# First-stage products issued in pairs on borrowed PSUM banks, and the middle column of x taken once a batch

## The chip, the cores and the metric

The kernel runs on one core of one Trainium2 chip. The metric is the device time of one execution in microseconds (us). The kernel before has a median of 1967.06 us over three runs (1964.94 to 1967.59). One more execution was recorded by the hardware profiler, and all times below that carry a position ("at 344.28") are microseconds from the start of that recorded span.

## The reference

```python
def _attn_ref(x):                 # x: 8 batches x 3008 rows x 256 columns, float32
    X = np.fft.fft(x, axis=1)
    X = np.fft.fft(X, axis=2)
    return X.real.astype(np.float32)

def _moe_ref(x, w_in, w_out):     # the 24064 rows of the result, w_in 256x2048, w_out 2048x256
    h = x @ w_in
    g = h * np.cos(h)
    return (g @ w_out).astype(np.float32)
```

The real part of a two-dimensional Fourier transform of each batch is followed by a two-layer network whose activation is h times cos(h). Everything is float32.

## The kernel before

The transform over the 3008 rows is split as 47 x 64. For each batch there is a **first stage**: the input is loaded in four parts of eight values of the row index modulo 64 (`load_x`, L140, four to six DMAs each on SyncE's queue), GpSimd folds columns d and 256-d into sums and differences (`fold`, L211; on VectorE for batch 0, ScalarE copies column 0 and the middle column 128), and `first_half` (L232) multiplies one chunk of four index values by the DFT matrix `L`. One chunk gives a PSUM tile `pz` of 128 x 512: its lower 64 partitions come from the sums ("even"), its upper 64 from the differences ("odd"). Since the weights have only 64 columns, the even and the odd products use different column halves of the array. A third, tiny product puts the middle column of x, which belongs to the even part, into the four odd columns that would be zero; it goes first. Chunk 0 has a column with weights of its own and needs six products. There are eight chunks a batch. ScalarE copies `pz` to `zs`, `store_z` (L265) writes it to DRAM, `load_z` reads it back transposed, and `second_half` (L289) makes the 225 or 256 columns of a *group* with four 128x128 products into `pb`; there are six groups a batch.

The **network** runs over 8 batches x 6 groups x 8 blocks of 256 hidden columns: 384 steps, each of two half-steps `k` (128 hidden columns). The main loop writes out by hand, for every engine, what belongs to half-step k: on TensorE `mm1(cur, 0)` (the row "H<-pq,WC"), three products of `mm2` of the step five half-steps back (rows "M<-..."), `mm1(cur, 1)` ("H<-pq,WS"), and on odd k one more `mm2` product. On ScalarE: `act_e` (ew<-H), `act_round` (r<-H), `seed` of the next half-step (H<-nb,wn: it writes the start value into the PSUM bank that the next `mm1` adds to), `act_sin` (r<-r). On VectorE: `dve_g` of half-step k-2 (L508), `dve_frac` (L498), `dve_h` (L482), and `take_m` at group ends. GpSimd makes the sums `S` (L524 to L531). The tail of each odd half-step holds output stores and the calls of `transform(b + 1)` (L330), a table from step number to calls: so the transform of the next batch is spread over the steps of this one. Every engine works its instructions in the order written.

The order of the work around the change: in `transform`, part p of x is loaded at step 8p and folded at 8p+6, 8p+7, 8p+9 and 8p+10; chunk 2p is multiplied at 8p+9 and stored at 8p+10, chunk 2p+1 at 8p+12 and 8p+13. PSUM has eight banks, four with the tag "M" for `mm2`, four with the tag "H" in a ring: seeds, `pz` and `pb` take the next bank of that ring in turn. In float32 each product of the program stands in the trace as two passes of TensorE ("x2" in a row).

The opening (batch 0) does the first stage before the loop and on "M" banks, and mixes loads of the weights and of the second DFT matrix `BJ` into the queue; the load of batch 1's part 0 is called at the end of step 0.

Of the kernel before, what the change touches and what calls it, by code (L numbers as in the profile page):

```python
# [11 lines left out]
FP = mybir.dt.float32  # L12
# [6 lines left out]
ND = 256  # L19
NDFF = 2048  # L20
N2 = 47
NJ = 24
NI = 32
IP = 4
NCH = NI // IP
XP = 2 * IP
NG = 6
# [81 lines left out]
def kernel(  # L109
# [87 lines left out]
    WS = cpool.tile([128, NDFF], FP, tag="WS", name="WS")  # L197
    wn = cpool.tile([128, 16], FP, tag="wn", name="wn")

    bank = {"M": 4, "H": 4}  # L200

    def psum(name, tag="H"):
        return ppool.tile([128, 512], FP, tag=tag, bufs=bank[tag], name=name)


    xfs = {}
# [22 lines left out]

    zss = {}  # L230

    def first_half(b, c):  # L232

        rows = 2 * N2 if b else 128
        fv = xfs.pop((b, c)).rearrange("r (e c) -> r e c", e=2)[0:rows]
        LE, LO, LE0, LO0 = (L[0:rows, 64 * q : 64 * q + 64] for q in range(4))
        pz = psum("pz", "H" if b else "M")
        pv = pz.rearrange("y (i d) -> y i d", d=128)
        xv = fv.rearrange("r e (i d) -> r e i d", d=128)
        parts = ((0, 1, LE0, LO0), (1, IP, LE, LO)) if c == 0 else ((0, IP, LE, LO),)  # L240

        def mul(e, i0, i1, d0, d1, w, rhs, start):
            nc.tensor.matmul(  # L243
                pv[64 * e : 64 * e + 64, i0:i1, d0:d1],
                lhsT=w,
                rhs=xv[:, rhs, i0:i1, d0:d1],
                start=start,
                stop=True,
                skip_group_check=True,
            )  # L250

        for i0, i1, wE, wO in parts:
            mul(1, i0, i1, 0, 1, wE, 1, i0 == 0)
        for i0, i1, wE, wO in parts:
            mul(0, i0, i1, 0, 128, wE, 0, i0 == 0)
            mul(1, i0, i1, 1, 128, wO, 1, False)
        tag, n = ("zs", 4) if b or c < 4 else ("pq", 8)
        zs = spool.tile([128, 512], FP, tag=tag, bufs=n, name="zs")
        nc.scalar.copy(out=zs, in_=pz)
        zss[b, c] = zs  # L260

    zds = {}
    z2s = {}
# [25 lines left out]
    def second_half(b, g):  # L289

        T = _width(g)
        z2 = z2s[b]
        pb = psum("pb", "H" if b or g else "M")
        for q in range(4):
            jj = 4 * g + q
            nc.tensor.matmul(  # L296
                pb[:, 128 * q : 128 * q + 128],
                lhsT=z2[:, jj * 128 : jj * 128 + 128],
                rhs=BJ[:, jj * 128 : jj * 128 + 128],
                start=q == 0,  # L300
                stop=True,
                skip_group_check=True,
            )
        pq = spool.tile([128, 512], FP, tag="pq", bufs=8, name="pq")
        pv = pq[:, 0 : 2 * T].rearrange("d (e t) -> d e t", e=2)
        bv = pb.rearrange("d (q e k) -> d e q k", q=4, e=2)
        if g == 0:
            nc.scalar.copy(
                out=pv[:, :, 0:192].rearrange("d e (q k) -> d e q k", k=64), in_=bv[:, :, 1:4, :]
            )  # L310
            nc.scalar.copy(out=pv[:, :, 192:225], in_=bv[:, :, 0, 0:33])
        else:
            nc.scalar.copy(out=pv.rearrange("d e (q k) -> d e q k", k=64), in_=bv)
        nb = spool.tile([128, 256], FP, tag="nb", bufs=8, name="nb")
        ready[b, g] = (pq, nb)
        if b == 0 and g == 0:
            return
        nd = dpool.tile([1, 256], FP, tag="nd", bufs=4, name="nd")
        nc.sync.dma_start(out=nd[:, 0:T], in_=pq[0:1, T : 2 * T])
        nc.sync.dma_start(out=nb[:, 0:T], in_=nd[0:1, 0:T].to_broadcast([128, T]))  # L320


    def spread_nb():
# [3 lines left out]
        nc.tensor.matmul(pn[:, 0:T], lhsT=ones, rhs=pq[0:1, T : 2 * T], start=True, stop=True)  # L327
        nc.scalar.copy(out=nb[:, 0:T], in_=pn[:, 0:T])

    def transform(b):  # L330
        todo = {}

        def at(o, *call):
            todo.setdefault(o, []).append(call)

        for p in range(4):
            at(8 * p, load_x, b, p)
            for c, o, f in ((2 * p, 6, 9), (2 * p + 1, 9, 12)):
                at(8 * p + o, fold, b, c, 0)
                at(8 * p + o + 1, fold, b, c, 1)  # L340
                at(8 * p + f, first_half, b, c)
                at(8 * p + f + 1, store_z, b, c)
        at(23, load_z, b, 0)
        at(39, load_z, b, 1)
        for g in range(NG):
            at(42 + g, second_half, b, g)
        return todo
# [142 lines left out]
    def act_round(h):  # L490
        if h.u == 0:
            h.s.r = spool.tile([128, 1024], FP, tag="r", bufs=4, name="r")
        r, y = sides(h)
        nc.scalar.activation(out=r, in_=y, func=AF.Copy, bias=BIG, scale=1.0)  # L494
# [7 lines left out]
    def act_sin(h):  # L502
        r, _ = sides(h)
        nc.scalar.activation(out=r, in_=r, func=AF.Sin, bias=0.0, scale=SIN_SCALE)  # L504
# [31 lines left out]
    def mm2(s, lo, hi, order=range(7)):  # L536
        T = s.T
        key = (s.b, s.grp)
        if s.fp == 0 and lo == 0:
            acc[key] = []  # L540
            started[key] = set()
        gv, sv = blocks(s)
        todo = (
            (0, wv[:, 0, 0, s.fp], gv[:, 0, 0]),
            (1, wv[:, 1, 0, s.fp], gv[:, 1, 0]),
            (2, vx[:, 3, s.fp], gv[:, 1, 1]),
            (3, vx[:, 1, s.fp], sv[:, 0]),
            (4, vx[:, 0, s.fp], sv[:, 1]),
            (5, vx[:, 2, s.fp], sv[:, 2]),
            (6, wv[:, 1, 1, s.fp], sv[:, 3]),  # L550
        )
        for m, w, a in (todo[i] for i in order[lo:hi]):
            first = m // 2 not in started[key]
            if first:
                acc[key].append(psum("M", "M"))
            started[key].add(m // 2)
            nc.tensor.matmul(  # L557
                acc[key][m // 2][:, 256 * (m % 2) : 256 * (m % 2) + T],
                lhsT=w,
                rhs=a,  # L560
                start=first,
                stop=s.fp == 7,
                skip_group_check=True,
            )
# [196 lines left out]
    for b in range(NB):  # L761
        for g in range(NG):
            for fp in range(8):
                s = Step()
                s.b, s.grp, s.fp, s.T = b, g, fp, _width(g)
                steps.append(s)
    per = NG * 8
    n = len(steps)

    def step(t, last=None):  # L770
# [14 lines left out]
    for k in range(2 * n + LAG):  # L785
        t, u = divmod(k, 2)
        d, v = divmod(k - LAG, 2)
        cur, prev, old, nxt = unit(k), unit(k - 1), unit(k - 2), unit(k + 1)
        done = step(d)
        full = step(d if v else d - 1, True)  # L790
        if cur:
            if k % (2 * per) == 0:
                todo = transform(cur.s.b + 1) if cur.s.b + 1 < NB else {}
            if k not in range(3, AHEAD):
                mm1(cur, 0)
                if t == 0:
                    seed_first(cur)
                act_e(cur)
            if k == 0:
                spread_nb()  # L800
                fold_weights(1, 3)
            elif k == 1:
                pw = weights(0, 3)
            elif k == 2:
                pw = weight_row(3)
        if done:
            order = (0, 1, 5, 4, 3, 2, 6) if done is steps[-1] else range(7)
            mm2(done, 4 * v, 4 * v + 3, order)
        if old:
            dve_g(old)  # L810
            if old.u:
                sums(old.s)
        if full and full is not steps[-1]:
            take_m(full, 1 if v else 3, nc.vector)
        if nxt and 0 < k < AHEAD - 1:
            seed(nxt)
        if prev:
            act_round(prev)
        if nxt and k >= AHEAD - 1:
            seed(nxt)  # L820
        if full and full is not steps[-1]:
            take_m(full, 0 if v else 2, nc.scalar)
        if prev:
            dve_frac(prev)
        if k + 1 in range(3, AHEAD):
            mm1(nxt, 0)
            act_e(nxt)
        if prev:
            act_sin(prev)
        if k == 1:  # L830
            keep_weights(0, 3, pw)
        elif k == 2:
            keep_wn(3, pw)
        if cur:
            mm1(cur, 1)
        if done and v == 0:
            mm2(done, 3, 4, order)
        if cur:
            dve_h(cur)
        if u == 0:  # L840
            continue
        for i in range(6):
            s = step(t - 4 - i, True)
            if s:
                combine_m(s, i)
        for sg, lag in ((0, 8), (1, 10)):
            s = step(t - lag, True)
            if s:
                store_out(s, sg)
        for call in opening.pop(t, ()):  # L850
            call[0](*call[1:])
        for call in todo.pop(t % per, ()):
            call[0](*call[1:])
# [31 lines left out]
```

## Time and profile before

| what | value |
|---|---|
| median of three runs | 1967.06 us |
| the profiled execution | 1965.9 us |
| its span, first to last instruction | 1964.1 us (1.8 us of the execution lie around it) |
| mean granted TensorE clock | 0.998 |
| VectorE / ScalarE / GpSimd busy | 1466.5 / 1497.9 / 1396.6 us |
| DMA | 88.71 MB, mean 45 GB/s |

A row of a timeline gives the start, the length, the engine, the line of the kernel, the operation, output tile <- input tiles, the shape and the number of instructions merged into it; in brackets stands idle time before it and what ended it. PE is TensorE's products, PEld its weight loads. A pass's recorded length holds the drain of the array as well, so two passes overlap in the records, and the cost of a pass is read from one start to the next.

### The profile page before, as it was taken

What the parts mean: (1) busy time and instruction counts of PE and PEld (TensorE: products, weight loads), DVE (VectorE), ACT (ScalarE), POOL (GpSimd) and SP (SyncE); (2) the same over time, 40 slices, a digit from 0 to 9 for tenths busy, and PEclk for the clock granted to TensorE, in tenths of its full rate; (3) what the DMA queues carried; (4) which work ended last, traced back from release to release, by engine and by line L of the source; (5) the groups of instructions that cost most, each with busy time, mean ns of one, the idle gap of its engine ahead of it and who ended that gap; (6) DMA issues with size and microseconds to landing.
All of it is one profiled execution on the core that took longest, in us unless ns stands there. A gap on an engine that the chain in (4) does not pass through costs nothing.

```text
span 1964.1 us, 29636 instructions
## 1 busy us (share of the span) xinstructions
PE 1950.2 (99%) x9360; PEld 1688.6 (86%) x9360; DVE 1466.5 (75%) x2522; ACT 1497.9 (76%) x3359; POOL 1396.6 (71%) x1593
## 2 busy tenths in 40 slices
PE   8999999999999999999999999999999999999998
PEld 4988889888988889888898888988889888898887
DVE  3777778777777777777777777777777777778786
ACT  3777778777777777777777777777777777778775
POOL 3777767777677866787668776687767777666775
PEclk9999999999999999999999999999999999999999
DMA  8412022121211312112221221113111231100001
GB/s 198 98 41 56 22 51 49 38 51 35 52 38 34 57 40 44 35 36 56 42 41 35 50 50 37 38 40 66 29 39 37 55 58 24 38 22 16 12 16 29
DMA packets 176690, 88.71 MB, mean 45 GB/s; under 512 B 103303, under 2 KB 173622, under 8 KB 174902
## 3 DMA queue, kind: packets, MB, share of 16 engines
q1 hardware_dynamic: 176374, 86.68, 21.5%
q8 instruction: 76, 1.25, 0.3%
q14 instruction: 80, 0.66, 0.1%
q10 hardware_dynamic: 160, 0.13, 0.0%
HBM read 49.50 MB, written 37.27 MB: 44 GB/s over the span
## 4 chain that ended last, share of the span: by engine, by line
PE 98%; DMA 1%; ACT 0%; DVE 0%; SPq 0%; POOL 0%; issue 0%; POOLq 0%; ACTq 0%
PE M L557 58%; PE H L466 34%; PE pz L243 3%; PE pb L296 2%; DMA xp<-in_x_dram 1%; PE pw L357 0%; PE pd L413 0%; DMA wr<-in_moe_w_in_dram 0%; DVE r L498 0%; ACT r L504 0%; DVE cb L624 0%; ACT r L494 0%; ACT H L447 0%; POOL xf L226 0%; PE H L453 0%
## 5 line engine op out<-in xcount | busy, mean ns | idle before, releaser
L524 POOL TENSOR_TENSOR S<-r 128x512 f32<-128x512 f32 (+1 forms) x383 | 475.0, 1240 | 461.2 <-DVE r L508 435.4
L498 DVE SCALAR_TENSOR_TENSOR r<-r,H 128x512 f32<-128x512 f32 (+1 forms) x768 | 518.8, 676 | 259.8 <-ACT r L494 232.3
L504 ACT ACTIVATE r<-r 128x512 f32<-128x512 f32 (+1 forms) x768 | 477.7, 622 | 264.2 <-DVE r L498 262.3
L557 PE MATMUL M<-S,VX 128*128 128x256 f32 (+1 forms) x2304 | 612.3, 375 | 0.0
L508 DVE SCALAR_TENSOR_TENSOR r<-H,r 128x512 f32<-128x512 f32 (+1 forms) x768 | 519.1, 676 | 120.9 <-ACT r L504 67.8
L557 PEld LDWEIGHTS M<-S,VX 128*128 128x128 f32 x2304 | 437.7, 190 | 50.0
L466 PE MATMUL H<-pq,WC 128*128 128x256 f32 (+1 forms) x1536 | 458.5, 380 | 2.1 <-ACT H L447 2.1
L466 PE MATMUL H<-pq,WS 128*128 128x256 f32 (+1 forms) x1536 | 450.6, 375 | 0.0
L494 ACT ACTIVATE r<-H 128x512 f32<-128x512 f32 (+1 forms) x768 | 448.0, 583 | 0.4 <-DVE H L482 0.4
L482 DVE TENSOR_TENSOR H<-ew,H 128x256 f32<-128x256 f32 (+1 forms) x768 | 325.0, 423 | 89.5 <-PE H L466 17.5
L557 PE MATMUL M<-r,w 128*128 128x256 f32 (+1 forms) x1536 | 388.4, 375 | 0.0
L447 ACT ACTIVATE H<-nb,wn 128x256 f32<-128x256 f32 (+1 forms) x766 | 366.3, 478 | 0.0
L466 PEld LDWEIGHTS H<-pq,WC 128*128 128x128 f32 x1536 | 277.0, 190 | 83.6 <-issue 42.8
L478 ACT ACTIVATE ew<-H 128x256 f32<-128x256 f32 (+1 forms) x768 | 289.1, 376 | 75.5 <-PE H L466 66.7
L557 PEld LDWEIGHTS M<-r,w 128*128 128x128 f32 x1536 | 301.0, 197 | 27.2
L466 PEld LDWEIGHTS H<-pq,WS 128*128 128x128 f32 x1536 | 291.4, 190 | 32.7 <-issue 0.7
L530 POOL TENSOR_TENSOR S<-S,r 128x256 f32<-128x256 f32 (+1 forms) x383 | 275.4, 719 | 30.0
L531 POOL TENSOR_TENSOR S<-r,S 128x256 f32<-128x256 f32 (+1 forms) x383 | 274.7, 717 | 30.0
L557 PE MATMUL M<-r,VX 128*128 128x256 f32 (+1 forms) x768 | 225.6, 375 | 0.0
L557 PE MATMUL M<-S,w 128*128 128x256 f32 (+1 forms) x768 | 225.2, 375 | 0.0
L557 PEld LDWEIGHTS M<-S,w 128*128 128x128 f32 x768 | 150.5, 196 | 14.7
L557 PEld LDWEIGHTS M<-r,VX 128*128 128x128 f32 x768 | 146.1, 190 | 14.6
(62 smaller groups left out, 916.4 us busy)
## 6 DMA issues: line engine op xcount, KB each, us to landing
out_dram<-ob SPq DMA_DIRECT2D x728, 32.0 KB
xp<-in_x_dram SPq DMA_DIRECT2D x56, 256.0 KB
zd<-zs SPq DMA_DIRECT2D x112, 96.0 KB
z<-zd SPq DMA_DIRECT2D x28, 384.0 KB
xp<-in_x_dram SPq DMA_DIRECT2D x56, 120.0 KB
nb<-nd SPq DMA_DIRECT2D x40, 128.0 KB
wr<-in_moe_w_in_dram SPq DMA_DIRECT2D x8, 256.0 KB
w<-in_moe_w_out_dram SPq DMA_DIRECT2D x4, 512.0 KB
```

What stands on the lines that cost most here:

```text
L447: nc.scalar.activation(out=h.H[:, 0:T], in_=s.nb[:, 0:T], func=AF.Copy, bias=0.25, scale=wn[:, f : f + 1])
L466: nc.tensor.matmul(h.H[:, 0:T], lhsT=W[:, 128 * f : 128 * f + 128], rhs=s.pq[:, e * T : e * T + T], start=False, stop=True, skip_group_che ...
L478: nc.scalar.mul(out=h.ew[:, 0:T], in_=h.H[:, 0:T], mul=2.0)
L482: nc.vector.tensor_tensor(out=h.H[:, T : 2 * T][:, ::-1], in0=h.ew[:, 0:T], in1=h.H[:, 0:T], op=ALU.subtract)
L494: nc.scalar.activation(out=r, in_=y, func=AF.Copy, bias=BIG, scale=1.0)
L498: nc.vector.scalar_tensor_tensor(out=r, in0=r, scalar=-BIG, in1=y, op0=ALU.add, op1=ALU.subtract)
L504: nc.scalar.activation(out=r, in_=r, func=AF.Sin, bias=0.0, scale=SIN_SCALE)
L508: nc.vector.scalar_tensor_tensor(out=r, in0=y, scalar=-0.25, in1=r, op0=ALU.add, op1=ALU.mult)
L524: tt(out=sv[:, 0:2], in0=qv[:, 1:2].to_broadcast([128, 2, T]), in1=qv[:, 0:4:3], op=ALU.subtract,)
L530: tt(out=sv[:, 2], in0=sv[:, 1], in1=gv[:, 0, 0], op=ALU.subtract)
L531: tt(out=sv[:, 3], in0=gv[:, 1, 0], in1=sv[:, 2], op=ALU.add)
L557: nc.tensor.matmul(acc[key][m // 2][:, 256 * (m % 2) : 256 * (m % 2) + T], lhsT=w, rhs=a, start=first, stop=s.fp == 7, skip_group_check=True,)
```

## The change

The middle column is no longer multiplied chunk by chunk for batches 1 to 7. `take_middle` copies column 128 of each loaded part into `xm` (ScalarE), `middle` multiplies all 32 columns of a batch at step 10 (two products into a cleared quarter of a bank) and copies the result to `zm`, and `keep_z` copies four values of it over the odd part of each chunk's `zs`. Parts of x are therefore loaded at steps 0, 2, 4 and 6, and `take_middle` stands two steps behind each load. `first_half` now issues the even product and then the odd one over all 512 columns (chunk 0: two each); batch 0 still has its tiny product, now behind them. Chunks 2p and 2p+1 are multiplied as a pair in the first half-step of step 8p+12, right behind `mm1(cur, 0)` and ahead of the `mm2` products; `pz` and `pb` no longer take a turn of the ring, but borrow the banks that the next seeds will use. The two `keep_z` of a pair stand ahead of the next seed and behind the sine. The steps of the four folds stay 8p+6, 8p+7, 8p+9 and 8p+10.

```diff
--- before.py
+++ after.py
@@ -197,10 +197,18 @@
     WS = cpool.tile([128, NDFF], FP, tag="WS", name="WS")
     wn = cpool.tile([128, 16], FP, tag="wn", name="wn")
 
-    bank = {"M": 4, "H": 4}
+    bank = {"M": 4, "H": 1}
+    turn = [0]
 
     def psum(name, tag="H"):
-        return ppool.tile([128, 512], FP, tag=tag, bufs=bank[tag], name=name)
+        at = tag
+        if tag == "H":
+            at = f"H{turn[0] % 4}"
+            turn[0] += 1
+        return ppool.tile([128, 512], FP, tag=at, bufs=bank[tag], name=name)
+
+    def borrow(name, k=0):
+        return ppool.tile([128, 512], FP, tag=f"H{(turn[0] + k) % 4}", bufs=1, name=name)
 
 
     xfs = {}
@@ -229,35 +237,70 @@
 
     zss = {}
 
-    def first_half(b, c):
+    def first_half(b, c, pz=None):
 
         rows = 2 * N2 if b else 128
         fv = xfs.pop((b, c)).rearrange("r (e c) -> r e c", e=2)[0:rows]
         LE, LO, LE0, LO0 = (L[0:rows, 64 * q : 64 * q + 64] for q in range(4))
-        pz = psum("pz", "H" if b else "M")
-        pv = pz.rearrange("y (i d) -> y i d", d=128)
-        xv = fv.rearrange("r e (i d) -> r e i d", d=128)
-        parts = ((0, 1, LE0, LO0), (1, IP, LE, LO)) if c == 0 else ((0, IP, LE, LO),)
-
-        def mul(e, i0, i1, d0, d1, w, rhs, start):
+        pz = pz or psum("pz", "M")
+        a = 128 if c == 0 else 0
+        for e, (w, w0) in enumerate(((LE, LE0), (LO, LO0))):
+            rows = slice(64 * e, 64 * e + 64)
+            if a:
+                nc.tensor.matmul(
+                    pz[rows, 0:128], lhsT=w0, rhs=fv[:, e, 0:128], start=True, stop=True
+                )
             nc.tensor.matmul(
-                pv[64 * e : 64 * e + 64, i0:i1, d0:d1],
+                pz[rows, a:512],
                 lhsT=w,
-                rhs=xv[:, rhs, i0:i1, d0:d1],
-                start=start,
+                rhs=fv[:, e, a:512],
+                start=not a,
                 stop=True,
                 skip_group_check=True,
             )
-
-        for i0, i1, wE, wO in parts:
-            mul(1, i0, i1, 0, 1, wE, 1, i0 == 0)
-        for i0, i1, wE, wO in parts:
-            mul(0, i0, i1, 0, 128, wE, 0, i0 == 0)
-            mul(1, i0, i1, 1, 128, wO, 1, False)
+        if b:
+            return pz
+        if a:
+            nc.tensor.matmul(
+                pz[64:128, 0:1], lhsT=LE0, rhs=fv[:, 1, 0:1], start=True, stop=True
+            )
+        nc.tensor.matmul(
+            pz[64:128, a:512:128],
+            lhsT=LE,
+            rhs=fv[:, 1, a:512:128],
+            start=True,
+            stop=True,
+        )
+        keep_z(b, c, pz)
+
+    def keep_z(b, c, pz):
         tag, n = ("zs", 4) if b or c < 4 else ("pq", 8)
         zs = spool.tile([128, 512], FP, tag=tag, bufs=n, name="zs")
         nc.scalar.copy(out=zs, in_=pz)
+        if b:
+            nc.scalar.copy(out=zs[64:128, 0:512:128], in_=zm[64:128, IP * c : IP * c + IP])
         zss[b, c] = zs
+
+    xm = cpool.tile([128, NI], FP, tag="xm", name="xm")
+    zm = cpool.tile([128, NI], FP, tag="zm", name="zm")
+
+    def take_middle(b, p):
+        xv = xs[b, p].rearrange("r (i d) -> r i d", d=ND)[0 : 2 * N2]
+        nc.scalar.copy(out=xm[0 : 2 * N2, XP * p : XP * p + XP], in_=xv[:, :, 128])
+
+    def middle(b):
+        pm = borrow("pm")[64:128, 0:NI]
+        nc.vector.memset(pm, 0.0)
+        for i0, i1, q in ((0, 1, 2), (1, NI, 0)):
+            nc.tensor.matmul(
+                pm[:, i0:i1],
+                lhsT=L[0 : 2 * N2, 64 * q : 64 * q + 64],
+                rhs=xm[0 : 2 * N2, i0:i1],
+                start=False,
+                stop=True,
+                skip_group_check=True,
+            )
+        nc.scalar.copy(out=zm[64:128], in_=pm)
 
     zds = {}
     z2s = {}
@@ -290,7 +333,7 @@
 
         T = _width(g)
         z2 = z2s[b]
-        pb = psum("pb", "H" if b or g else "M")
+        pb = borrow("pb") if b or g else psum("pb", "M")
         for q in range(4):
             jj = 4 * g + q
             nc.tensor.matmul(
@@ -327,6 +370,9 @@
         nc.tensor.matmul(pn[:, 0:T], lhsT=ones, rhs=pq[0:1, T : 2 * T], start=True, stop=True)
         nc.scalar.copy(out=nb[:, 0:T], in_=pn[:, 0:T])
 
+    pairs = {}
+    per = NG * 8
+
     def transform(b):
         todo = {}
 
@@ -334,12 +380,14 @@
             todo.setdefault(o, []).append(call)
 
         for p in range(4):
-            at(8 * p, load_x, b, p)
-            for c, o, f in ((2 * p, 6, 9), (2 * p + 1, 9, 12)):
-                at(8 * p + o, fold, b, c, 0)
-                at(8 * p + o + 1, fold, b, c, 1)
-                at(8 * p + f, first_half, b, c)
-                at(8 * p + f + 1, store_z, b, c)
+            at(2 * p, load_x, b, p)
+            at(2 * p + 2, take_middle, b, p)
+            for k in range(4):
+                at(8 * p + (6, 7, 9, 10)[k], fold, b, 2 * p + k // 2, k % 2)
+            pairs[per * (b - 1) + 8 * p + 12] = b, 2 * p
+            for c in (2 * p, 2 * p + 1):
+                at(8 * p + 12, store_z, b, c)
+        at(10, middle, b)
         at(23, load_z, b, 0)
         at(39, load_z, b, 1)
         for g in range(NG):
@@ -764,7 +812,6 @@
                 s = Step()
                 s.b, s.grp, s.fp, s.T = b, g, fp, _width(g)
                 steps.append(s)
-    per = NG * 8
     n = len(steps)
 
     def step(t, last=None):
@@ -803,19 +850,27 @@
                 pw = weights(0, 3)
             elif k == 2:
                 pw = weight_row(3)
-        if done:
-            order = (0, 1, 5, 4, 3, 2, 6) if done is steps[-1] else range(7)
-            mm2(done, 4 * v, 4 * v + 3, order)
+        pair = None if u else pairs.pop(t, None)
+        if pair:
+            b, c = pair
+            pz = [first_half(b, c, borrow("pz"))]
         if old:
             dve_g(old)
             if old.u:
                 sums(old.s)
+        if pair:
+            pz.append(first_half(b, c + 1, borrow("pz", 1)))
+        if done:
+            order = (0, 1, 5, 4, 3, 2, 6) if done is steps[-1] else range(7)
+            mm2(done, 4 * v, 4 * v + 3, order)
         if full and full is not steps[-1]:
             take_m(full, 1 if v else 3, nc.vector)
         if nxt and 0 < k < AHEAD - 1:
             seed(nxt)
         if prev:
             act_round(prev)
+        if pair:
+            keep_z(b, c, pz[0])
         if nxt and k >= AHEAD - 1:
             seed(nxt)
         if full and full is not steps[-1]:
@@ -827,6 +882,8 @@
             act_e(nxt)
         if prev:
             act_sin(prev)
+        if pair:
+            keep_z(b, c + 1, pz[1])
         if k == 1:
             keep_weights(0, 3, pw)
         elif k == 2:
```

## The prediction

> **What bounds the kernel now.** I read the page first (busy time, slices, chain), then TensorE's timeline around one `pz`, then SyncE's and ScalarE's timelines where a load of x is due, and the stretches with DMA share and clock.
>
> ```profile
> PE 1950.2 (99%) x9360; PEld 1688.6 (86%) x9360; DVE 1466.5 (75%) x2522; ACT 1497.9 (76%) x3359; POOL 1396.6 (71%) x1593
> PE 98%; DMA 1%; ACT 0%; DVE 0%; SPq 0%; POOL 0%; issue 0%; POOLq 0%; ACTq 0%
> PE M L557 58%; PE H L466 34%; PE pz L243 3%; PE pb L296 2%; DMA xp<-in_x_dram 1%; PE pw L357 0%; PE pd L413 0%; DMA wr<-in_moe_w_in_dram 0%; DVE r L498 0%; ACT r L504 0%; DVE cb L624 0%; ACT r L494 0%; ACT H L447 0%; POOL xf L226 0%; PE H L453 0%
> ```
>
> TensorE is the bound, and the chain hardly ever leaves it. So each nanosecond that the change takes from TensorE is a gain, and each wait that it brings to TensorE a loss. One chunk on TensorE:
>
> ```profile
> 343.32 0.59 PE L466 MATMUL H<-pq,WS 128*128 128x256 f32 x2
> 343.75 0.59 PE L557 MATMUL M<-S,VX 128*128 128x256 f32 x2
> 344.28 1.18 PE L243 MATMUL pz<-xf,L 94*64 94x4 f32 x6
> 345.39 0.70 PE L466 MATMUL H<-pq,WC 128*128 128x256 f32 x2
> 345.93 0.81 PE L557 MATMUL M<-S,VX 128*128 128x256 f32 x3
> ```
>
> From start to start a 256-column product takes 0.43 us. From 343.75 to 345.93 there are two of them (0.86) and the chunk, so a chunk costs 1.31 us; the records repeat this for every chunk within 2 ns. The single starts inside are: middle column 344.278 and 344.357, even 344.285 and 344.765, odd 344.415 and 344.871, next full product 345.390. Even and odd run side by side in the two column halves. Of the 1310 ns, 93 are the entry (309 from the last full pass instead of 216), 137 the middle column ahead of the odd passes, 456 the step between odd passes, 519 the last pass with its way out, and 104 a weight load laid bare behind it; the two streams of 512 columns would need 858.
>
> **What goes (TensorE).** A pair enters and leaves once instead of twice and has no middle. In the opening two chunks stand next to each other, and the even half runs on from 9.977 to 10.406 (429 ns); so I take chunks as seamless and each further pass at 456 to 480, 470 as the mean. A pair then costs 93 + 3 x 470 + 15 (second half's start) + 519 + 104 = 2140 ns against 2620: 480 less. The pair with chunk 0 had a block of 1432 (the block at 568.15) + 1310 and gives about 570. Per batch 570 + 3 x 480 = 2.0 us, for seven batches **-14.0 us** (12 to 15.5). Batch 0 has its tiny product behind instead of ahead: nothing.
>
> The Trainium skill ("TensorEngine Tiling (Array Packing)", Key Properties) says that a change of tiling mode drains TensorE; the trace agrees (309 for 216 going in), and the rule by itself would count five ins and outs a batch instead of eight, without a price.
>
> **What hides.** The second `pz` needs the bank of half-step k-2, read last by `dve_g`. In an even half-step that ends 1.02 us behind the start of `mm1(cur, 0)` (339.44 to 340.46), and the second chunk starts 1.46 us behind it (0.43 + 0.09 + 0.94): no wait, 0.44 us to spare; late by more, it would hold the `mm2` products queued behind, 28 times. ScalarE gets two copies of 0.59 and two small ones (0.19, as L226) in one half-step, 1.55 us, while TensorE is 2.1 us longer in it; the seed follows the first copy and is over about 1.5 us before its product. The ring's freed turn changes nothing that TensorE saw. Folds keep their steps; SyncE's stores of a pair go out together, with load_z three steps behind.
>
> **What comes (TensorE).** `middle` waits at the end of step 10 for a memset that stands behind `dve_h` on VectorE. In an odd half-step `dve_h` ends 0.20 us past the point where the next `mm1` would start (364.69 against 364.49); a memset of 32 columns is about 0.09 (246 ns for 225 columns, 485 for 512). Then four short passes at 58 to 79, way out and bare weight load (0.2): 0.77 us a batch. In batch 1 `pb` borrows the same bank just before, so the memset waits for ScalarE's copy too: 1.4. Sum **+6.0** (4.3 to 8). The skill (same page, Instruction Overhead) gives each matmul about 60 cycles; the trace's 58 to 79 ns a pass decide.
>
> **What comes (ScalarE waits for x).** Each `take_middle` waits on ScalarE for the load two steps before, and everything behind it in that queue waits too: `act_e`, the seed, and with them TensorE's next `mm1`. Before, the first reader of a load was a fold six steps behind, on GpSimd. First the load of batch 1's part 0, issued behind the opening's big loads:
>
> ```profile
> 55.28 0.34 SPq L151 DMA_DIRECT2D xp<-in_x_dram  x1
> 53.25 0.58 ACT L504 ACTIVATE r<-r 128x450 f32<-128x450 f32 x1 [0.35 <-DVE r L498]
> 54.99 0.36 ACT L478 ACTIVATE ew<-H 128x225 f32<-128x225 f32 x1 [1.16 <-PE H L466]
> 62.00:63.00 1.00, 1.00 (x8) 1.00 (x7) 0.88 (x2) 0.65 (x3) 0.95 (x1) 1.00 0.60 79
> 63.00:64.00 1.00, 1.00 (x7) 0.99 (x6) 0.66 (x2) 0.99 (x3) 0.84 (x3) 1.00 0.08 18
> 64.00:65.00 1.00, 1.00 (x7) 0.95 (x6) 0.75 (x3) 0.65 (x3) 1.00 (x2) 1.00 0.01 2
> 65.00:66.00 1.00, 1.00 (x7) 1.00 (x6) 0.83 (x2) 1.00 (x3) 0.92 (x2) 1.00 0.00 0
> ```
>
> The last of its six transfers is issued at 55.28 (the stretches' last two columns are DMA share and GB/s: traffic ends at about 64), and its last completion signal is recorded at 64.60. In the instruction order of the changed program this `take_middle` stands between the sine of 53.25 and the ew of 54.99. So that ew starts at about 64.85, 9.85 us late; the seed behind it delays the product of half-step 7 (before: 56.32) as much, less 0.1. TensorE has nothing else. **+9.75** (8.5 to 11.5, if the parts queued behind slow it). Then the clock:
>
> ```profile
> 46.90:50.30 3.40, 1.36 (x6) 1.01 (x7) 2.60 (x5) 3.07 (x8) 1.97 (x3) 1.00 1.24 187
> 50.30:53.70 3.40, 3.40 (x11) 3.05 (x10) 2.17 (x4) 2.24 (x6) 1.49 (x2) 0.50 1.18 196
> ```
>
> A stretch of 3.4 us in which TensorE worked 1.36 was followed by one at half clock. A gap of 9.75 should do that too; counted on in 3.4 us from 50.30, TensorE resumes at 66.1 inside a stretch that ends at 67.4, the next at 70.8. Half clock to 67.4 costs 0.65, to 70.8 costs 2.35. A full busy stretch ended it above, so nearer to the latter: **+2.0**. The Trainium skill ("TensorE: Matmul & The Clock Gate", Part 1) says the same: half rate after an idle window of about 3.4 us, full after a busy one. This rule speaks against the change.
>
> Later batches, part 0 (batch 4 shown):
>
> ```profile
> 773.76 0.40 SPq L151 DMA_DIRECT2D xp<-in_x_dram  x1
> 774.67 6.43 SPq L686 DMA_DIRECT2D out_dram<-ob  x8
> 778.44 0.58 ACT L504 ACTIVATE r<-r 128x450 f32<-128x450 f32 x1
> 778.93 0.34 ACT L478 ACTIVATE ew<-H 128x225 f32<-128x225 f32 x1
> 780.10 0.65 PE L466 MATMUL H<-pq,WC 128*128 128x225 f32 x2
> ```
>
> The copy would stand behind the sine that ends at 779.02, but the last signal comes at 779.48, and ScalarE has no idle time here (ew starts under the sine's end, and the product of 780.10 is already held by its seed). The ew moves by 0.75, TensorE with it. Batches 2 to 7 by their signals: 0.15, 0.8, 0.75, 0.55, 0.8 and 0.3: **+3.3** (2.3 to 4.5). Part 1 is issued behind the eight stores that end at 781.10, 11.9 us behind the start of step 1 (769.21); a part took 6.3 to 6.8 us from first issue to last signal, so it is there at 18.5. ScalarE reaches its copy at 17.9, plus part 0's delay, with 0.2 to spare behind: 0 to 0.5 a batch, and up to 1 if part 2, queued right behind, slows it. I take **+2.0** (0 to 6). Parts 2 and 3 have four more microseconds each: nothing. The plain copies (0.19 each, 28, where ScalarE idles 0.14 to 0.35 a half-step): **+0.3**.
>
> **Sum.** -14.0 + 6.0 + 9.75 + 2.0 + 3.3 + 2.0 + 0.3 = +9.3 us on the profiled 1965.9, 1975.2; the median of the runs lies 1.2 above the profiled execution, so 1976.
>
> **Rivals.**
> - *The waits for x don't reach TensorE* (faster): the loads are there when ScalarE comes. Then -14.0 + 6.0 + 0.3 = -7.7: 1959. It decides at 54.0 for batch 1 and about 0.5 us before the last signals later. Against it: 64.60. For it: only that the order on SyncE may shift in ways the old trace does not show. Chance 0.07.
> - *Only the opening is paid*: part 0 a little sooner or ScalarE less tight, so that 3.3 and 2.0 fall away: +4.0, 1971. For it: margins of tenths. 0.13.
> - *The chunks of a pair don't join* (the change doesn't do what it says): a drain or a late weight load between them, so that only the middle's 137 ns x 56 and 122 ns more for each chunk 0 go, -8.5 instead of -14.0: 1982. 0.05.
> - *ScalarE's pile in the pair's half-step holds the seeds*: with 0.75 us on each of 28 pairs, +21: 1997. The 1.5 us to spare speak against it. 0.05.
> - The forecast: 0.70.
>
> **How the numbers follow.** A measurement of this kernel can tell about 0.2% (3.9 us) from no change. The terms' bounds spread the forecast over some 1969 to 1983; the range 1967 to 1984 takes in the second and third rivals and leaves out 1959, 1997 and the tails, about 2 in 10. Faster than 1963.1: the first rival and a tail, 0.08. Within 0.2%: half of the second and the forecast's lower tail, 0.13. Slower: 0.79.
>
> **What would show it.** In the changed profile: blocks of `pz` with 8 passes and about 2.14 us each in place of two of 1.31; a pause of TensorE of about 10 us from 56, ended by ScalarE's `xm` copy waiting for DMA of x, and half clock behind it; about 0.8 us lost by each `pm`; waits of `xm` under 1 us in steps 2 and 4 of later batches. No pause near 56 would make the prediction wrong, and so would idle TensorE inside or behind the pairs.

## The result and the profile after

The changed kernel takes 1976.75 us (median of four runs, 1976.52 to 1978.06) against 1966.63 us for the kernel before on the same chip: ratio 1.0054, 95% interval 1.0036 to 1.0071, about 10 us slower. The forecast was 1976. The profiled execution took 1976.83 us with a span of 1975.0, 10.9 us more than the span before.

The page of the changed kernel, busy time and the chain by engine:

```profile
PE 1944.0 (98%) x9262; PEld 1688.1 (85%) x9262; DVE 1455.9 (74%) x2529; ACT 1519.6 (77%) x3450; POOL 1398.4 (71%) x1593
PE 89%; DMA 4%; DVE 3%; ACT 2%; SPq 1%; issue 0%; POOL 0%; DVEq 0%; ACTq 0%; POOLq 0%
```

TensorE worked 6 us less in a span 11 us longer, and the chain now leaves it for a tenth of the time, to DMA, VectorE and ScalarE. TensorE's timeline around a pair:

```profile
631.73 0.59 PE L514 MATMUL H<-pq,WC 128*128 128x256 f32 x2
632.25 1.94 PE L253 MATMUL pz<-xf,L 94*64 94x512 f32 x8
634.12 0.92 PE L605 MATMUL M<-S,VX 128*128 128x256 f32 x3
```

The eight passes stand where two blocks of six stood. In single starts, the block takes 2177 ns from the second WC pass to the next M pass; less that WC pass's own 216, and with the bare weight load of 104 behind it, 2065 ns against 2620 before. Now the opening, ScalarE, the chain of waits, and TensorE behind the pause:

```profile
53.27 0.58 ACT L552 ACTIVATE r<-r 128x450 f32<-128x450 f32 x1 [0.45 <-DVE r L546]
64.83 0.20 ACT L289 COPY xm<-xp 94x8 f32<-94x8 f32 x1 [10.98 <-DMA xp<-in_x_dram]
64.94 0.35 ACT L526 ACTIVATE ew<-H 128x225 f32<-128x225 f32 x1
```
```profile
54.83 9.94 DMA xp<-in_x_dram
64.76 0.03 ACTq L289
64.79 0.04 issue
64.83 0.20 ACT xm L289
65.03 0.27 ACT ew L526
65.30 0.04 issue
65.34 1.89 PE H L514 x4
```
```profile
65.34 1.12 PE L514 MATMUL H<-pq,WS 128*128 128x225 f32 x2 [10.52 <-ACT ew L526]
67.02 1.71 PE L605 MATMUL M<-r,w 128*128 128x225 f32 x4
```

In the chain each row is a start, a length and what ran: load of x, its copy to `xm`, ew, product (ACTq is ScalarE's queue; "issue" is time for which the profile shows no wait). TensorE stood idle for 10.5 us, and behind that four passes of 225 columns take 1.50 us (67.02 to 68.52) where 0.76 is usual. The stretches (last three columns: clock, DMA share, GB/s) name the reason:

```profile
58.00:62.00 4.00, 0.00 (x0) 0.00 (x0) 0.00 (x0) 0.00 (x0) 0.00 (x0) 0.50 1.14 185
66.00:71.50 5.50, 5.50 (x16) 4.87 (x15) 2.94 (x6) 2.35 (x6) 3.62 (x5) 0.50 0.70 128
71.50:75.00 3.50, 3.50 (x20) 3.42 (x19) 2.12 (x4) 2.74 (x7) 0.54 (x2) 0.99 0.02 5
```

The clock is halved from 57.9 to 71.55. This is what the rule of the clock gate in the Trainium skill ("TensorE: Matmul & The Clock Gate", Part 1) had said for an idle window. Every other engine stands still in the pause too.

TensorE and VectorE around one `pm`:

```profile
585.12 0.59 PE L605 MATMUL M<-S,VX 128*128 128x256 f32 x2
586.37 0.42 PE L295 MATMUL pm<-xm,L 94*64 94x1 f32 x4 [0.65 <-DVE pm L293]
586.71 0.70 PE L514 MATMUL H<-pq,WC 128*128 128x256 f32 x2
```
```profile
584.83 0.39 DVE L630 TENSOR_SCALAR mr<-M 128x225 f32<-128x225 f32 x1
585.13 0.68 DVE L546 SCALAR_TENSOR_TENSOR r<-r,H 128x512 f32<-128x512 f32 x1
585.73 0.42 DVE L530 TENSOR_TENSOR H<-ew,H 128x256 f32<-128x256 f32 x1
586.23 0.09 DVE L293 MEMSET pm<- 64x32 f32 x1
```

TensorE waits for the memset, and VectorE is late with it because a `take_m` (mr<-M) of the group's end stands in the same half-step: the part of step 10 that the forecast did not see. A `pm` costs 1.27 us.

**The account**, by starts of passes in the two traces: pairs -16.3 us; `pm` +9.05 (1.46 in batch 1, six times 1.265); opening +12.55 (pause 10.7, and half clock 3.1 here where the old execution had 1.7 from 50.3; the rest is small differences ahead of the loop); products held elsewhere +5.55. Together 10.85 of the 10.9.

### The profile page after: what moved, and what is told of

Read it like the earlier page. It is cut to its first block, busy times and chain, and to the rows that moved or that the text cites. A ratio compares the mean times of both kernels' runs of the same rounds, so it can differ in the third digit from the quotient of the medians.

```text
span 1975.0 us, 29718 instructions
## 1 busy us (share of the span) xinstructions
PE 1944.0 (98%) x9262; PEld 1688.1 (85%) x9262; DVE 1455.9 (74%) x2529; ACT 1519.6 (77%) x3450; POOL 1398.4 (71%) x1593
## 4 chain that ended last, share of the span: by engine, by line
PE 89%; DMA 4%; DVE 3%; ACT 2%; SPq 1%; issue 0%; POOL 0%; DVEq 0%; ACTq 0%; POOLq 0%
PE M L605 53%; PE H L514 31%; PE pz L253 3%; DMA xp<-in_x_dram 2%; PE pb L339 2%; DVE r L546 1%; DMA zd<-zs 1%; ACT r L552 1%; DVE r L556 1%; ACT r L542 1%; DMA w<-in_moe_w_out_dram 0%; ACT ew L526 0%; DVE mr L630 0%; DMA wr<-in_moe_w_in_dram 0%; DMA out_dram<-ob 0%
```

## The experiments

All were run five rounds beside the kernel before, whose median was 1966.41 us beside e1 to e4, 1965.14 beside e5, e6, e8 and e9, and 1966.24 beside e10 and e11. Versions from different calls are therefore compared by their ratios.

**Who pays for the waits.** Theory: ScalarE waits for x in `take_middle`, and TensorE waits for ScalarE. Rivals: the early loads cost by themselves, or the pairs do.

e1:

```diff
-            at(2 * p + 2, take_middle, b, p)
+            at(6 + p, take_middle, b, p)
```

> The changed kernel with the four take_middle of a batch moved to steps 6, 7, 8 and 9 (they stood at 2, 4, 6 and 8). Theory (ScalarE waits for x and TensorE with it): the pause of 11 us and the half clock behind it at 54 to 71, together 12.4 us net, go, and so do the late products in step 2 of batches 2 to 7, 3 to 4 us: about 1960.5, below the kernel before. Rival (the early loads cost by themselves, or the pairs and the extra ScalarE copies do): 1972 or more.

Measured: 1961.78 us, ratio 0.9976 (0.9967 to 0.9985): 15 us less than the changed kernel, from four small copies a batch that stand later. No wait of `xm` for a load is left. Its profiled execution shows no half clock in the opening at all, neither the changed kernel's nor the 3.4 us of the kernel before; where the low stretch falls varies from execution to execution, and 1.7 us of such differences belong to that.

e2 (the kernel before with the loads early):

```diff
-            at(8 * p, load_x, b, p)
+            at(2 * p, load_x, b, p)
```

> The kernel before with the four loads of x at steps 0, 2, 4 and 6 instead of 0, 8, 16 and 24, and nothing else. Theory: a load by itself costs nothing, since the folds still read it at step 6 or later: 1966.6, within 1 us. Rival (the early loads crowd the queue of the stores, or the DMA engines): 3 to 10 us slower.

Measured: 1967.48 us, ratio 1.0007 (0.9998 to 1.0016). No change lies in the interval, which ends at 0.16%, 3 us; so the early loads don't make the changed kernel's loss. But they are not free. Once, in the opening, TensorE waits for a seed, and the seed for a small transfer to `nb` that now stands behind more loads of x:

```profile
77.21 0.48 ACT L447 ACTIVATE H<-nb,wn 128x256 f32<-128x256 f32 x1 [1.34 <-DMA nb<-nd]
77.74 0.70 PE L466 MATMUL H<-pq,WC 128*128 128x256 f32 x2 [0.85 <-ACT H L447]
```

By starts that is 1.1 us, as much as the medians differ. e1 has the same wait, with TensorE idle for 2.34 us until 78.14; in the changed kernel nothing is lost there.

e5 (late in batch 1 alone):

```diff
-            at(2 * p + 2, take_middle, b, p)
+            at(6 + p if b == 1 else 2 * p + 2, take_middle, b, p)
```

> The changed kernel with take_middle late (steps 6 to 9) in batch 1 alone; batches 2 to 7 keep theirs at steps 2, 4, 6 and 8. Theory: the opening's pause and its half clock (12.4 us net in the profile) go, the late products in step 2 of batches 2 to 7 stay (about 3.5 us): 1964.5, between the kernel before and the version with all of them late. Rival (the later waits are the larger part): 1970 or more.

Measured: 1965.47 us, ratio 0.9999 (0.9991 to 1.0008). Against the changed kernel's 1.0054 the opening alone is worth 0.55%, 10.8 us; the rest up to e1, 0.23% or 4.5 us, is the wait in later batches (3.5 us by starts in the changed trace). In the changed profile that wait looks like this for batch 3, on ScalarE and then on TensorE:

```profile
550.03 0.58 ACT L552 ACTIVATE r<-r 128x450 f32<-128x450 f32 x1
551.67 0.20 ACT L289 COPY xm<-xp 94x8 f32<-94x8 f32 x1 [1.06 <-DMA xp<-in_x_dram]
```
```profile
552.18 0.65 PE L514 MATMUL H<-pq,WS 128*128 128x225 f32 x2 [0.81 <-ACT ew L526]
```

The profile puts three waits of ScalarE down to x (12.6 us in all, 11.0 of it in the opening, the others in batches 3 and 5). Two more in front of `xm` (0.48 us in batch 6, 0.14 in batch 2) it puts down to a store of the output, which shares a semaphore with the loads; in batch 6 the last signal of part 0 is recorded at 1270.30, 0.09 us ahead of the copy, so that this too is a wait for x. TensorE loses 0.35, 1.27, 0.30, 0.80, 0.69 and 0.10 us in batches 2 to 7. Where the wait is short, the copy itself costs, since it stands in a step where ScalarE has no idle time.

**The clock.** e6 adds work for TensorE in the pause:

```diff
+    def fill():
+        pd = borrow("pd")
+        for i in range(20):
+            nc.tensor.matmul(pd[:, 0:256], lhsT=VX[:, 0:128], rhs=BJ[:, 0:256], start=i == 0, stop=i == 19)
...
+        if b == 1:
+            at(2, fill)
```

> The changed kernel with 20 products of 256 columns (8.6 us of TensorE at full clock, into a borrowed bank, read by nobody) at the end of step 2, where TensorE idles for 11 us. Theory (the pause itself is ScalarE's, the clock falls because TensorE idles): the pause lasts as long, to about 65, but the products behind it run at full clock, 0.19 us apart instead of 0.37: 2.8 us less, 1974. Rival (the low clock is not due to idling): no change, 1976.7, or slower by the added products if the pause was shorter than they are.

Measured: 1976.74 us (1974.39 to 1978.09), ratio 1.0054 (1.0042 to 1.0067). TensorE's timeline in its profile:

```profile
53.94 8.80 PE L379 MATMUL pd<-BJ,VX 128*128 128x256 f32 x40
66.71 0.65 PE L527 MATMUL H<-pq,WS 128*128 128x225 f32 x2 [2.45 <-ACT ew L539]
67.97 0.92 PE L618 MATMUL M<-r,w 128*128 128x225 f32 x4
68.73 0.54 PE L618 MATMUL M<-r,VX 128*128 128x225 f32 x2
```

The passes behind the pause run at full speed (67.97 to 68.73 for four), so the half clock was due to idling; the mean granted clock, 0.997 to 0.998 in the five executions against 0.995 to 0.996 in the changed kernel's, agrees. But the median did not fall by 2.8 us, and a step of that size, 0.14%, would lie within the two intervals. The copy waited until 66.20 in this execution, 1.4 later than in the changed kernel's, which accounts for half of it there; this execution also had a half-clock stretch at 24.8, in the first stage of batch 0. Whether that is why x came later stays open. In the changed kernel's trace the half clock costs 3.1 us by starts; that the total falls by as much without it is not shown.

**The pairs.** e3 has pairs, and a tiny product per chunk behind the odd one:

```diff
-        if b:
-            return pz
         if a:
             nc.tensor.matmul(
                 pz[64:128, 0:1], lhsT=LE0, rhs=fv[:, 1, 0:1], start=True, stop=True
             )
...
+        if b:
+            return pz
         keep_z(b, c, pz)
...
-        if b:
-            nc.scalar.copy(out=zs[64:128, 0:512:128], in_=zm[64:128, IP * c : IP * c + IP])
...
-            at(2 * p, load_x, b, p)
-            at(2 * p + 2, take_middle, b, p)
+            at(8 * p, load_x, b, p)
...
-        at(10, middle, b)
```

> Pairs on borrowed banks alone: the tiny product of the middle column is kept for each chunk (behind the odd product, as batch 0 of the changed kernel has it), no xm, no pm, no zm copies, loads at steps 0, 8, 16 and 24. Theory: a pair's block costs 2.07 us plus two tiny products of 0.14, against 2.62 for two chunks apart, 0.28 less, 28 times and a little for chunk 0: about 8 us below the kernel before, 1958.5. Rival (the gain in the pair's block comes from the missing tiny products): 1964 or more.

Measured: 1958.80 us, ratio 0.9962 (0.9949 to 0.9976). This kernel and e4 below leave out a part of the sum: their last starting product covers only part of a bank of the ring, and part of the seeds of later half-steps no longer enters h (argued from the program; no run isolates it). Number, shape and order of the instructions are as told. e10 has the old three products and old loads, and nothing but the pairs (against the kernel before, without the changes to the banks and the main loop that the pairs need):

```diff
-        pz = psum("pz", "H" if b else "M")
+        pz = pz or psum("pz", "M")
...
-                at(8 * p + f, first_half, b, c)
+            pairs[per * (b - 1) + 8 * p + 12] = b, 2 * p
```

> The kernel before with the pairs on borrowed banks and nothing else: each chunk keeps its three products in the old order (tiny product of the middle column first), loads at steps 0, 8, 16 and 24, no xm, pm or zm. Theory: ways in and out saved once per pair and seamless chunks make a block about 0.37 us shorter than two chunks apart, 28 times 0.37 = 10.4, less about 2 for ScalarE's exposed copies in step 8p + 10: 8 us below the kernel before. Rival (the gain hangs on the new form of the products): less than 4 us.

Measured: 1959.27 us, ratio 0.9966 (0.9954 to 0.9978), 6.7 us below the kernel before; its block is 2390 ns, or 2278 by the same working, against 2620. So the gain of the pairs hangs neither on the new form of the products nor on `middle`; the tiny products add 0.21 us a pair, and 28 of these, 6 us, are all that `middle` can save, at a price of 9.05 in the changed kernel. At the lowest price found below, 0.545 us each in e9, some 2 us would be left, and the ratios of e9 and e10 (0.9964 and 0.9966) don't show them.

**What pm waits for.** e4 has no memset:

```diff
-        nc.vector.memset(pm, 0.0)
...
-                start=False,
+                start=i0 == 0,
```

> The changed kernel without the memset of pm: the first of the two products of middle starts the bank, the second adds to it where nothing has been written. Theory (TensorE waits for the memset, which stands behind dve_h on VectorE): of 1.27 us per pm in batches 2 to 7 only way in, four short passes, way out and one bare weight load are left, 0.54; batch 1 still waits for the copy of pb: 4.4 us less than the changed kernel, 1972.3. Rival (it waits for the bank to come free): no change, 1976.7.

Measured: 1973.09 us, ratio 1.0036 (1.0024 to 1.0049). The waits ahead of `pm` fell from 5.2 to 0.75 us in the traces, and the 0.75 stand in batch 1, where `pb` borrows the same bank just before. So in the other six batches it was the memset, not the bank. e8, with `take_middle` late, moves `middle` past the step with `take_m`:

```diff
-        at(10, middle, b)
+        at(11, middle, b)
```

> take_middle late in all batches, and middle at step 11 instead of 10, where VectorE has no take_m of a group's end and no pb uses the same bank. Theory (what TensorE waits for is how far dve_h is behind, and take_m put it 0.4 us further back): 0.77 us per pm as forecast instead of 1.27, 0.5 x 7 = 3.7 us less than the version with take_middle late (1961.8): 1958.1. Rival (the wait is the same in any step): 1961.8.

Measured: 1959.40 us, ratio 0.9970 (0.9958 to 0.9982). By starts a `pm` now costs 0.87 us in all seven batches, against 1.46 once and 1.31 six times in e1; that is 3.2 us less in the trace, with profiled spans of 1957.2 and 1960.9. The wait for `nb` in the opening, shorter by 1.6 us in this execution, and 0.18 us a batch that TensorE now loses in step 11, before hidden behind `pm`, are further parts of that difference. The ratios of e1 and e8 differ by only 0.06%, less than either interval. e9 clears earlier (against e8):

```diff
+    def clear_pm(b):
+        pms[b] = borrow("pm", 1)[64:128, 0:NI]
+        nc.vector.memset(pms[b], 0.0)
+
     def middle(b):
-        pm = borrow("pm")[64:128, 0:NI]
-        nc.vector.memset(pm, 0.0)
+        pm = pms[b]
...
+        mids[per * (b - 1) + 11] = b
...
             if old.u:
                 sums(old.s)
+        if u and t in mids:
+            clear_pm(mids.pop(t))
```

> As the version with middle at step 11, but the memset of pm stands behind dve_g of the same half-step, ahead of dve_h. Theory: nothing is left to wait for, a pm costs way in, four short passes, way out and a bare weight load, 0.54 us; (1.27 - 0.54) x 7 = 5.1 us less than the version with take_middle late: 1956.5. Rival (the bank or ScalarE's copies hold it): 1958 or more.

Measured: 1957.61 us, ratio 0.9964 (0.9951 to 0.9976); a `pm` costs 0.545 us, the floor that was expected. The fall of the total is less sure: the ratio is 0.12% below that of e1, within the intervals.

**What is left.** In all pair versions so far, e3 and e10 without `xm` too, TensorE loses 0.1 us up to three times a batch in step 8p + 11, between the two passes of a product. ScalarE's timeline ahead of it has `mr<-M` and the fold's copy in one step, and no idle time. e11 is e9 with the second chunk's folds a step earlier:

```diff
-                at(8 * p + (6, 7, 9, 10)[k], fold, b, 2 * p + k // 2, k % 2)
+                at(8 * p + (6, 7, 8, 9)[k], fold, b, 2 * p + k // 2, k % 2)
```

> The version with the early memset, and the second chunk's folds at steps 8p + 8 and 8p + 9 instead of 8p + 9 and 8p + 10. Theory (in step 8p + 10 ScalarE has take_m of a group's end and the fold's copy of column 0, and without the old chunk's extra time on TensorE they hold the seed by 0.1 us, and a weight load by 0.1 more now and then): 0.1 us x 3 x 7 = 2.1 us less than 1957.6, 1955.5. Rival (GpSimd with a fold more in step 8p + 8 is late with the sums): slower.

Measured: 1955.56 us, ratio 0.9945 (0.9933 to 0.9958), and the 0.1 us are gone from the trace. This version is 0.55% faster than the kernel before, and so faster than both kernels.

## Why the prediction was right, point by point

- **Entry and exit once per pair** (-14.0, bounds 12 to 15.5): right in kind, too small; -16.3. The step that missed was "each further pass at 456 to 480, 470 as the mean": even and odd start 7 ns apart, and in each half the starts are 480, 429 and 430 ns apart. The kernel before has one step to a half and chunk, so its 480 was the step behind the way in, paid once per pair. It is not that its halves run 100 ns out of step: in e10 the odd half starts 131 ns behind the even one, and the even half's steps are 480, 430 and 429 all the same.
- **What hides**: right for the pair. The bank of k-2, ScalarE's two copies and the seeds hold nothing: every block of eight passes takes 2176 or 2177 ns, and every one with chunk 0 (twelve passes) 2188 or 2189.
- **middle** (+6.0, bounds to 8): +9.05. The term used `dve_h`'s end in a half-step without a `take_m`; e8 puts `pm` into such a step and measures 0.87 against the 0.77 forecast.
- **The opening** (+9.75 and +2.0): right in the chain of waits. The ew came 9.95 us late by its start (64.94 against 54.99); the pause is 10.7 because TensorE came to it sooner in this execution, and the product that waits is `mm1(cur, 1)` of half-step 6, not the next half-step's. The half clock cost more (3.1), but the 1.7 that the kernel before paid from 50.3 was missing here, which the forecast did not count; so the two terms together, 11.75, stand against 12.1, and that they meet is luck.
- **Part 0 later** (+3.3): about 3.5 in the trace, what is left of the 5.55 when the 2.1 of the fold's copies are taken off. The total is right, the batches are not: 0.35, 1.27, 0.30, 0.80, 0.69 and 0.10 us in 2 to 7, against 0.15, 0.8, 0.75, 0.55, 0.8 and 0.3. **Part 1** (+2.0): nothing; no copy behind part 0 waits.
- **The plain copies** (+0.3): 2.1, by another way than forecast. Not `xm` but the old fold's copy is exposed: e3 and e10 lose the same without `xm`, and in e11 the loss goes with the fold. That the chunk of step 8p + 9 used to give ScalarE 1.3 us of TensorE's time to catch up is argued, not shown.

So the sum was nearer than its terms: 2.3 us too little gain and 2.0 too much for part 1 against 3.05 and 1.8 too little loss. The forecast for the profiled execution, 1975.2, was 1.6 too low, and the 1.2 added for the median did not come again (profiled execution 1976.83, median 1976.75). That 1976 lies within 1 us of the result is in part luck.

## What to carry to other kernels

Before a reader is put two steps behind a load, compare the load's last completion signal in the old trace with the place of the new wait in its engine's queue: one copy of 0.2 us that waited on an in-order engine cost 10.8 us here, more than the 6.7 that the pairs alone gained. Loads that move ahead also hold up small transfers queued behind them. A gain on the bounding engine also takes cover from the others, so look for the next engine that has no idle time in the steps that become shorter. Split a change that mixes a gain and a loss; here the pairs alone were worth 0.34%.

## What the runs showed of the hardware that was not expected

Two streams in the two column halves run at the pace of one: behind a first step of 480 ns both halves of a pair go on at 429 to 430 ns a pass of 512 columns, where the full array takes 2 x 216 ns for as many. The low clock lasted from 57.9 to 71.55, 6.2 us past TensorE's return at 65.34, although TensorE was without a pause from there on; the forecast had counted 4.7. The half-clock stretches behind a pause in these traces last 3.41 us (the kernel before), 10.24 (e4, 60.0 to 70.24) and 13.65 (the changed kernel): one, three and four times 3.41.
